# Sliding-window attention with channel mix: the xr mixes of the first batch on GpSimd, re-searched instruction lists, and an earlier bank for the last piece

## The chip, the core and the metric

The kernel runs on one core of a Trainium2 chip. The core has TensorE (PE, whose weight loads appear as PEld), VectorE (DVE), ScalarE (ACT), GpSimd (POOL) and SyncE (SP), which work from their own instruction queues and meet through semaphores. Data goes between HBM and SBUF by DMA; matmul results go to PSUM, which has eight banks here. The metric is the device time in microseconds, as a median of several executions.

## The reference

The inputs q, k and v are [8, 8, 576, 64] (batch, head, position, head dimension). The first stage is causal attention in a window of 128 with ALiBi slopes, the second is an RWKV channel mix with d_model 512 and d_ff 1024.

```python
scores = scale * np.matmul(q, k.transpose(0, 1, 3, 2))
mask = (rel >= 0) & (rel < window)              # rel = query - key, window 128
attn = softmax(np.where(mask, scores + bias, -1e9))   # bias = -slope[head] * |rel|
x = np.matmul(attn, v)                          # -> [8, 576, 512]
x_prev = x shifted down by one position, zeros first
xk = mu_k * x + (1.0 - mu_k) * x_prev
xr = mu_r * x + (1.0 - mu_r) * x_prev
k = np.maximum(xk @ w_k, 0.0)                   # w_k [512, 1024]
v = k * k @ w_v                                 # w_v [1024, 512]
r = 1.0 / (1.0 + np.exp(-(xr @ w_r)))           # w_r [512, 512]
out = r * v
```

(The softmax line is shortened; the reference spells it out.)

## The kernel before

All matmuls are in bf16. A batch has 576 = 4 x 128 + 64 positions; the last 64 are called its tail.

**Attention, batch by batch.** q and k of a batch arrive by GpSimd's DMA queue (tile `cb`, the tails `ts`, the values `vs` and `tv`) and are turned by PE (`qk_quad`, `qk_some`, `tails`, the helper `transpose` at L397), or from batch 4 on by transposing DMAs of SP. ACT or DVE copies the turned blocks from PSUM to `qk`, `tt` or `qx` (`copy_any`, L715). `scores` (L742) multiplies two heads at a time, one in each 64-row half of the array; ACT takes the exponent (L766); the ALiBi factor and the mask are a DVE product with a table (L779), or for the first batch a bias matmul (L748) with the diagonal tiles `sid`. `attend` (matmuls at the helper line L394, `vs` with `at`) also sums the weights through a column of ones; DVE takes the reciprocal (L813) and scales (L819) into `xu`. PE transposes `xu` (L397), and ACT or DVE copies it to `xt` (through `copy_of`).

**`shift`** makes the channel mix's inputs of a head pair g: `dl` = x - x_prev (L906, DVE), then the two mixes `xk` = dl * mu_k + x_prev and `xr` = dl * mu_r + x_prev, each one DVE instruction (scalar_tensor_tensor, L913). Batch 0 is worked in two parts, positions 0 to 256 and 256 to 576, so it has eight xk mixes and eight xr mixes, of 256 and 320 elements a partition. In the first part `dl` of all four head pairs is kept in a spare output buffer (shown as `ot` in the profile), and the xr mixes are made after the last xk mix.

**`channel_mix`** works on two batches (a pair) in slices of columns. For each of eight slices of d_ff, four matmuls with `wk_sb` (a wk group), a relu (L994, ACT or DVE) and a square (L1000 and L1002) give `kk`. For each 128 output rows, four matmuls of 512 columns with `wr_sb` (a wr group) and a tanh on ACT (L1046) give `rs`, then two halves of four matmuls each with `wv_sb` (wv groups, the halves of d_ff) end in one DVE instruction (L1060) that makes `ot`, which SP stores (L1085). The last 128 rows are worked in two pieces of 384 and 128 columns (`FIN`), the second stored by ACT's queue (L1079). Each piece asks for its own PSUM bank when it starts.

**The order of the work.** `Plan` simulates the kernel's nodes (each a few instructions, with a duration, a latency, buffers that it needs and frees). PE, ACT and DVE work through lists written out in `ORDER`; a list's numbers count the nodes of these three engines in the order in which the program creates them, so a node's number in a list also decides which engine makes it where several may. GpSimd and SP take whatever is ready, lowest priority number first; a DMA's priority is its number among all nodes. GpSimd issues the loads (waiting, by the plan, for the eighth load before it to be done). A change between 64-row and 128-row operands on PE has a price of its own in the plan (`SWITCH`). The first loads, after q and k of the first part of batch 0, come in the order of the string below: v is values, K and k the two halves of w_k, a and b q/k of batch 1 and its tail, R w_r, W and w the two halves of w_v, c the values of batch 1; the loads of batch 2 follow.

```python
LOADS = 'v2tKVkabRWwc'
```

`WARM` lists column counts (in units of 128) of PE warm-up matmuls ahead of the first data.

Of the kernel before, what the change touches and what calls it, by code (L numbers as in the profile page):

```python
# [37 lines left out]
""".split()],  # L38
    "ACT": [int(x) for x in """
# [10 lines left out]
""".split()],  # L50
    "DVE": [int(x) for x in """
# [190 lines left out]
def kernel(  # L242
# [35 lines left out]
    WARM = (4, 4, 4, 4, 4, 4, 4, 1, 1)  # L278
# [42 lines left out]
    def XT(b, g):  # L321
        return XT0 if b < 2 else (ACT,)
# [35 lines left out]
    ident = cst.tile([128, 128], BF16, name="ident")  # L358
    mask = cst.tile([128, H, 512], BF16, name="mask")
# [50 lines left out]
    def dve_t(n, fast=1):  # L410
        return (n / fast + 66) / 960.0

    XRL = 4.0

# [370 lines left out]
    def attend(b, g, t0, t1, ha, deps, prio):  # L785
# [43 lines left out]
        r = op(DVE, 0.2, [a], prio + (0,), emit_r, [hx])  # L829
# [5 lines left out]
    def out_t(b, g, t0, t1, hx, deps, prio, hk, ht, late=None):  # L835
# [15 lines left out]
        x = op(XT(b, g), {ACT: act_t(n), DVE: dve_t(n)}, [o, virt_xt[b]], prio + (1,), lambda e: copy_of(  # L851
# [17 lines left out]
    def out_some(b, g, hx, deps, prio, ht):  # L869
# [7 lines left out]
        for r in range(2):  # L877
            nt = NJ - r

            def emit_c(e, r=r, nt=nt):  # L880
                copy_of(hp[r], e, xt_buf[ht.idx][:, g:g + m, X0:X0 + S].rearrange(
                    "p g (t c) -> p g t c", c=64)[:, :, r::2],
                    one(hp[r]).bitcast(BF16)[:, 0:64 * m * NJ].rearrange(
                        "p (g t c) -> p g t c", g=m, c=64)[:, :, 0:nt])
            xs.append(op(XT(b, g), {ACT: act_t(64 * m * nt), DVE: dve_t(64 * m * nt)},
                         [o, virt_xt[b]], prio + (1,), emit_c, (), [hp[r]]))
        return xs

    def shift(b, g, c0, c1, deps, prio, hk, ht, late=None):
# [19 lines left out]
        for i, (buf, mu, nm) in enumerate(((xk_buf, muk_sb, n_muk), (xr_buf, mur_sb, n_mur))):  # L909
            def mix(more=(), i=i, buf=buf, mu=mu, nm=nm):  # L910
                return op(DVE, dve_t(n) + 0.06, [d, nm, virt_x[b // 2]] + list(more),
# [94 lines left out]
    def channel_mix(P, c0, c1, first, xks, xrs, order):  # L1006
# [27 lines left out]
        for i, c in enumerate(range(c0 // 128, c1 // 128)):  # L1034
# [30 lines left out]
            for a, b in ((0, FIN), (FIN, 512)) if final else ((0, 512),):  # L1065
                if a:
                    hv = Hold("p")
# [262 lines left out]
```

## Time and profile before

| | |
|---|---|
| time, median of 3 | 225.93 us (225.9 to 226.34) |
| the profiled execution | 226.01 us, its span 224.0 us |
| granted TensorE clock | 1.00 |
| PE busy | 217.2 us, 97% of the span |
| PEld, DVE, ACT, POOL busy | 126.5, 187.1, 152.3, 92.1 us |
| chain of waits | PE 86%, DMA 8%, POOL 2% |
| DMA | 33.83 MB, 151 GB/s on average |

The span runs from the first to the last instruction that the profiler saw; 2.0 us of the execution lie around it. A line of the profile names the kernel's line, the engine, the operation and the tiles, written one first, and then the count. In the timeline, the first two numbers are the start and the length in us of a run of like instructions; matmuls are pipelined, so the length of a PE run reaches past the start of the next, and PE's prices are best taken from start to start. In the groups, what stands after the bar is the busy time of the group in us, the mean of one instruction in ns, and the idle time of the engine ahead of them with what ended it.

### The profile page before, as it was taken

To read this page: it belongs to the slowest core of one execution; us is meant where nothing else is said; L and a number is where in the kernel's file an instruction comes from. 1 tells how busy PE (TensorE), PEld (TensorE's weight loads), DVE (VectorE), ACT (ScalarE), POOL (GpSimd) and SP (SyncE) were. 2 spreads that over 40 slices of the span, in tenths; PEclk is the share of its full clock that TensorE was granted. 3 is DMA by queue.
4 is the path that set the end of the run, shared out by engine and by line. 5 is a ranking of instruction groups with operands and counts; after the bars stand their busy time and mean duration, and the time that the engine had idled before them with its cause. 6 is when DMAs were issued, how large, how long until landed. Compare 5 with 4: busy or idle time off the path is not lost.

```text
span 224.0 us, 6237 instructions
## 1 busy us (share of the span) xinstructions
PE 217.2 (97%) x2482; PEld 126.5 (56%) x2482; DVE 187.1 (84%) x426; ACT 152.3 (68%) x272; POOL 92.1 (41%) x118
## 2 busy tenths in 40 slices
PE   7899899999999999999999999999999999999994
PEld 2466665755776455557565554457744554574442
DVE  6678899999959999998999896899979999864232
ACT  3679899797989886983889943864448832475111
POOL 8964746589990992475425854300000000000000
PEclk9999999999999999999999999999999999999999
DMA  6999999999999999999999999999982183210243
GB/s 168 176 187 200 197 196 175 227 146 154 199 156 170 111 186 125 180 172 155 167 233 151 155 154 148 156 214 208 133 217 89 41 108 68 82 63 0 94 154 127
DMA packets 132092, 33.83 MB, mean 151 GB/s; under 512 B 119256, under 2 KB 127712, under 8 KB 132064
## 3 DMA queue, kind: packets, MB, share of 16 engines
q0 software_dynamic: 95728, 16.26, 96.0%
q1 hardware_dynamic: 34592, 16.59, 39.8%
q10 hardware_dynamic: 1744, 0.59, 1.1%
q8 instruction: 19, 0.31, 0.6%
q14 instruction: 9, 0.07, 0.1%
HBM read 33.56 MB, written 9.44 MB: 192 GB/s over the span
## 4 chain that ended last, share of the span: by engine, by line
PE 86%; DMA 8%; POOL 2%; ACT 1%; issue 1%; DVE 0%; POOLq 0%; ACTq 0%
PE duo L394 76%; PE duo L742 7%; DMA cb<-in_k_dram 5%; PE duo L397 3%; DMA qx<-in_k_dram 3%; POOL vs L518 1%; ACT qk L715 1%; ACT xt L715 0%; POOL qx L514 0%; POOL cb L514 0%; ACT rs L1046 0%; POOL dist L457 0%; POOL dist L465 0%; POOL dist L468 0%; DVE ot L1060 0%
## 5 line engine op out<-in xcount | busy, mean ns | idle before, releaser
L394 PE MATMUL duo<-xk,wk_sb 128*128 128x256 bf16 (+2 forms) x416 | 69.7, 314 | 0.3 <-DMA wk_sb<-in_moe_w_k_dram 0.3
L394 PE MATMUL duo<-wv_sb,kk 128*128 128x512 bf16 (+2 forms) x296 | 69.9, 374 | 0.1
L766 ACT ACTIVATE at<-duo 128x1024 bf16<-128x1024 f32 (+2 forms) x68 | 64.8, 1008 | 3.3 <-PE duo L742 3.1
L994 ACT ACTIVATE rl<-duo 128x384 bf16<-128x384 f32 (+2 forms) x94 | 42.9, 484 | 28.8 <-PE duo L394 25.1
L394 PEld LDWEIGHTS <-wk_sb 128*128 128x128 bf16 x416 | 38.7, 98 | 21.7 <-issue 0.6
L394 PEld LDWEIGHTS <-kk 128*128 128x128 bf16 x296 | 27.1, 98 | 29.9 <-issue 1.1
L1046 ACT ACTIVATE rs<-duo 128x512 bf16<-128x512 f32 x36 | 21.6, 613 | 27.2 <-PE duo L394 24.2
L779 DVE TENSOR_TENSOR at<-at,mask 128x1024 bf16<-128x1024 bf16 x56 | 37.3, 686 | 0.6 <-ACT at L766 0.6
L518 POOL DMA_DIRECT2D vs<-in_v_dram x32 | 28.4, 904 | 20.2 <-PE duo L394 16.8
L1060 DVE SCALAR_TENSOR_TENSOR ot<-rs,duo 128x512 f32<-128x512 bf16 (+2 forms) x37 | 24.3, 668 | 14.0 <-PE duo L394 8.5
L394 PE MATMUL duo<-wr_sb,xr 128*128 128x512 bf16 x144 | 35.7, 380 | 0.0
L1002 DVE TENSOR_TENSOR kk<-rl 128x256 bf16<-128x256 bf16 (+2 forms) x92 | 29.5, 335 | 6.0 <-ACT rl L994 5.7
L819 DVE TENSOR_TENSOR xu<-duo,rc 128x640 bf16<-128x640 f32 (+2 forms) x36 | 26.5, 743 | 0.3
L913 DVE SCALAR_TENSOR_TENSOR xr<-dl,mu_sb,xt 128x576 bf16<-128x576 bf16 (+1 forms) x32 | 25.0, 781 | 0.0
L913 DVE SCALAR_TENSOR_TENSOR xk<-dl,mu_sb,xt 128x576 bf16<-128x576 bf16 (+1 forms) x32 | 24.4, 780 | 0.1
L394 PEld LDWEIGHTS <-at 128*128 128x128 bf16 x576 | 21.4, 97 | 5.3 <-ACT at L766 0.3
L394 PE MATMUL duo<-vs,at 128*128 128x65 bf16 x512 | 21.8, 193 | 0.1
L394 PEld LDWEIGHTS <-xr 128*128 128x128 bf16 x144 | 13.3, 98 | 13.9
L549 POOL DMA_DIRECT2D cb<-in_q_dram x20 | 17.7, 921 | 4.9 <-DMA cb<-in_k_dram 1.9
L549 POOL DMA_DIRECT2D cb<-in_k_dram x20 | 17.8, 941 | 2.8 <-DMA vs<-in_v_dram 2.8
L906 DVE TENSOR_TENSOR dl<-xt 128x576 bf16<-128x576 bf16 (+1 forms) x32 | 13.6, 438 | 4.7 <-ACT xt L715 2.2
L715 ACT COPY qk<-duo 128x512 bf16<-128x512 bf16 (+1 forms) x32 | 16.0, 580 | 2.0 <-PE duo L397 2.0
(75 smaller groups left out, 177.5 us busy)
## 6 DMA issues: line engine op xcount, KB each, us to landing
out_dram<-ot SPq DMA_DIRECT2D x34, 256.0 KB, 4.8
vs<-in_v_dram POOLq DMA_DIRECT2D x32, 128.0 KB, 9.1
cb<-in_q_dram POOLq DMA_DIRECT2D x20, 128.0 KB, 8.4
cb<-in_k_dram POOLq DMA_DIRECT2D x20, 128.0 KB, 12.8
wk_sb<-in_moe_w_k_dram POOLq DMA_DIRECT2D x2, 512.0 KB, 9.1
cb<-in_q_dram POOLq DMA_DIRECT2D x4, 256.0 KB, 10.0
cb<-in_k_dram POOLq DMA_DIRECT2D x4, 256.0 KB, 10.2
wv_sb<-in_moe_w_v_dram POOLq DMA_DIRECT2D x2, 512.0 KB, 11.6
```

Of the source, the lines that this page charges most:

```text
L394: return use(h, nc.tensor.matmul(*a, **k))
L518: return dma(POOL, 256, issue_t(1024), lambda e: nc.gpsimd.dma_start(out=vs_buf[h.idx][:, j, :, 0:D], in_=v[b, :, 128 * j:128 * j + 128].r ...
L549: return [dma(POOL, 256, issue_t(1024), lambda e, r=r: nc.gpsimd.dma_start(out=cb_buf[h.idx][:, i, r], in_=src[:, :, r]), [g], kind="q") f ...
L715: return (nc.scalar.copy if e == ACT else nc.vector.tensor_copy)(out=out, in_=in_)
L766: lambda e, ah=ah, w=w, hp=hp: nc.scalar.activation(out=ah(), in_=two(hp)[:, :, 0:w], func=AF.Exp, scale=float(scale)), (), [hp])
L779: nc.vector.tensor_tensor(out=a, in0=a, in1=m, op=ALU.mult)
L819: use(hp, nc.vector.tensor_tensor(out=out_, in0=a5()[:, :, :, 0:D], in1=rc[:, :, 0:nt, None].to_broadcast([128, 2, nt, D]), op=ALU.mult), hx)
L913: lambda e: nc.vector.scalar_tensor_tensor(out=buf[hk.idx][:, g, e0 + c0:e0 + c1], in0=dls(), scalar=mu[:, g:g + 1], in1=xc(1), op0=ALU.mu ...
L994: return nc.scalar.activation(out=out, in_=in_, func=AF.Relu, scale=RELU_SCALE)
L1002: nc.vector.tensor_tensor(out=out, in0=in_, in1=in_, op=ALU.mult)
L1046: lambda e, hp=hp, hs=hs: use(hp, nc.scalar.activation(out=rs_buf[hs.idx], in_=one(hp), func=AF.Tanh, scale=0.5), hs), [hs], [hp])
L1060: use(hv, nc.vector.scalar_tensor_tensor(out=ot_buf[ho.idx][:, a:b], in0=rs_buf[hs.idx][:, a:b], scalar=1.0, in1=one(hv)[:, a:b], op0=ALU. ...
```

## The change

1. In `shift`, the eight xr mixes of batch 0 go to GpSimd: a product with mu into a new fp32 buffer `mix32` (128 x 320) and an addition of x_prev. All eight share the one buffer. The plan prices a pair at 0.0033 us an element + 0.4 and gives it the priority 500, that is, behind all DMAs with a lower number and ahead of those above; it isn't tied to the chain of GpSimd's DMAs.
2. All three lists are searched anew. PE's has 378 entries as before; ACT's goes from 277 to 259, DVE's from 426 to 436. Eight numbers fall out (the mixes), so that a new number from 100 on stands for an older one up to eight higher. The lists also move copies to `qk` and `xt`, relus and squares between ACT and DVE.
3. The copies to `xt` may be on either engine in every batch, not in the first two alone.
4. Planner prices: the reciprocal 0.135 us for 0.2, three kinds of copies from PSUM on DVE at the double rate, the cast of the first part on DVE 0.12 us dearer, and between the two halves of a wv product no latency.
5. The last piece's second PSUM bank is taken together with the first one, ahead of the first matmuls (`spare`).
6. The last warm-up entry is 2 for 1.

```diff
 ORDER = {
     "PE": [int(x) for x in """
-39 40 41 42 43 44 45 46 50 52 47 53 64 66 90 88 67 76 91 78 55 79 93 58 37 81 96 161 69 158 107 84 124 104 162
-110 72 111 141 164 113 114 165 127 128 144 145 130 147 148 131 116 167 150 203 197 170 206 133 200 255 119 153
-191 185 136 267 300 194 270 253 188 222 240 273 214 303 258 288 209 228 237 216 261 217 306 291 294 211 225 212
-276 264 219 309 248 297 408 279 231 243 234 411 312 245 394 441 429 246 414 250 396 432 435 251 333 330 324 342
...
+39 40 41 42 43 90 52 50 44 45 46 53 47 64 88 76 66 91 78 79 55 93 154 67 81 58 96 37 69 103 151 84 106 72 155
+100 107 157 109 110 135 119 158 125 141 138 139 112 160 122 142 123 126 195 163 144 189 198 115 128 259 147 131
+247 177 262 292 192 245 280 180 183 186 265 295 206 201 298 250 208 253 220 229 232 283 209 286 211 203 214 256
+268 301 204 400 226 271 235 289 217 421 223 386 403 240 304 406 388 433 237 242 243 424 436 427 238 367 319 325
...
-    WARM = (4, 4, 4, 4, 4, 4, 4, 1, 1)
+    WARM = (4, 4, 4, 4, 4, 4, 4, 1, 2)
...
     def XT(b, g):
-        return XT0 if b < 2 else (ACT,)
+        return XT0
...
+    mix32 = cst.tile([128, 320], FP32, name="mix32")
...
+    XMIX = 500
...
-        r = op(DVE, 0.2, [a], prio + (0,), emit_r, [hx])
+        r = op(DVE, 0.135, [a], prio + (0,), emit_r, [hx])
...
             def mix(more=(), i=i, buf=buf, mu=mu, nm=nm):
+                if b == 0 and i:
+                    def both(e):
+                        nc.gpsimd.tensor_scalar(out=mix32[:, 0:n], in0=dls(), scalar1=mu[:, g:g + 1],
+                                                scalar2=None, op0=ALU.mult)
+                        nc.gpsimd.tensor_tensor(out=buf[hk.idx][:, g, e0 + c0:e0 + c1],
+                                                in0=mix32[:, 0:n], in1=xc(1), op=ALU.add)
+
+                    return plan.add(POOL, n * 0.0033 + 0.4, 0.25, [d, nm, virt_x[0]], (XMIX,), both,
+                                    (), [hd, ht])
...
                 if a:
-                    hv = Hold("p")
+                    hv = spare
+                elif final:
+                    spare = Hold("p")
                 for half in range(2):
                     m = op(PE, NPO * mm(b - a), squares[4 * half:4 * half + 4] +
-                           [n_wv[half], m], place(),
+                           [n_wv[half], (m, 0.0)], place(),
                            lambda e, f=emit2, h=half, a=a, b=b, hv=hv: f(
                                e, 4 * h, 4 * h + 4, a, b, hv),
-                           [hv] if half == 0 else [], [hk])
+                           [hv, spare] if final and not a and half == 0 else
+                           [hv] if not a and half == 0 else [], [hk])
```

More of the change, by code (lines that the diff above doesn't have):

```diff
@@ L850, in out_t @@
         o = op(PE, 0.0565 * (t1 - t0), deps, prio + (1,), emit, [hp], [hx])
-        x = op(XT(b, g), {ACT: act_t(n), DVE: dve_t(n)}, [o, virt_xt[b]], prio + (1,), lambda e: copy_of(
+        x = op(XT(b, g), {ACT: act_t(n), DVE: dve_t(n, 2)}, [o, virt_xt[b]], prio + (1,), lambda e: copy_of(
             hp, e, xt_buf[ht.idx][:, g, X0 + c0:X0 + c1], tp()[:, c0:c1]), (), [hp])
@@ L884, in emit_c @@
                         "p (g t c) -> p g t c", g=m, c=64)[:, :, 0:nt])
-            xs.append(op(XT(b, g), {ACT: act_t(64 * m * nt), DVE: dve_t(64 * m * nt)},
+            xs.append(op(XT(b, g), {ACT: act_t(64 * m * nt), DVE: dve_t(64 * m * nt, 2)},
                          [o, virt_xt[b]], prio + (1,), emit_c, (), [hp[r]]))
@@ L947, in tails_full @@
         g = virtual("tt", [htt])
-        c = [op(DVE, dve_t(512), [t, g], prio + (0,), emit_c, (), [hp])]
+        c = [op(DVE, dve_t(512, 2), [t, g], prio + (0,), emit_c, (), [hp])]
         return htt, c
@@ L1147 @@
                 for i in range(2):
-                    cs.append(op(CAST, {ACT: act_t(256, True), DVE: dve_t(256, 2) + 0.08},
+                    cs.append(op(CAST, {ACT: act_t(256, True), DVE: dve_t(256, 2) + 0.2},
                                  src0[i, g], prio + (0,), lambda e, i=i, g=g: copy_any(
```

71 rows, old and new, of the table ORDER are left out of this document.

## The prediction

> **What bounds the kernel now.** I read the table of windows first, then the waits of TensorE, then its timeline around the places where the two PE lists differ. The windows split the span at 32 and 220 us; the columns are window, length, then busy us (and instructions) of PE, PEld, DVE, ACT and POOL, the granted clock, the DMA share and GB/s.
>
> ```profile
> 0.00:32.00 32.00, 28.32 (x491) 17.62 (x492) 25.00 (x97) 23.98 (x51) 21.45 (x33) 1.00 1.41 188
> 32.00:220.00 188.00, 188.00 (x1984) 108.43 (x1985) 161.27 (x329) 128.03 (x222) 70.68 (x85) 1.00 1.39 145
> 220.00:224.00 4.00, 0.90 (x10) 0.49 (x8) 0.84 (x2) 0.32 (x1) 0.00 (x0) 1.00 0.37 131
> ```
>
> TensorE is busy all 188.00 us from 32 to 220, at clock 1.00. It sat idle for 32.00 - 28.32 = 3.68 us at the start, and the last 4 us are the drain. So the end moves only with the idle time of the start, with waits that appear later, with work that PE gets more of, and with the drain. What DVE, ACT or GpSimd save elsewhere buys nothing by itself. The early waits of PE, largest first (total us, times, longest):
>
> ```profile
> PE duo L394 <- DVE xt L482: 1.0, 1, 1.0
> PE duo L742 <- ACT qk L715: 0.6, 2, 0.3
> PE duo L397 <- DMA cb<-in_k_dram: 0.5, 1, 0.5
> ```
>
> The three give 2.1 us. The attractive reading is: relieve DVE early, and PE gets these back. What a saved microsecond is worth depends on what PE meets next, so here is the stretch of PE's timeline in which batch 0 ends (start, length with the pipeline's end, line, tiles, count).
>
> ```profile
> 32.80 1.04 PE L394 MATMUL duo<-xk,wk_sb 128*128 128x256 bf16 x8
> 33.68 1.03 PE L394 MATMUL duo<-wv_sb,kk 128*128 128x512 bf16 x4
> 34.63 0.34 PE L742 MATMUL duo<-qk 64*128 64x256 bf16 x4
> 34.81 0.19 PE L742 MATMUL duo<-tt,qk 64*128 64x64 bf16 x2
> 34.84 0.19 PE L742 MATMUL duo<-tt 64*128 64x64 bf16 x2
> 34.97 1.04 PE L394 MATMUL duo<-wv_sb,kk 128*128 128x512 bf16 x4
> ...
> 37.65 0.60 PE L394 MATMUL duo<-xk,wk_sb 128*128 128x256 bf16 x4
> 38.09 1.03 PE L394 MATMUL duo<-wv_sb,kk 128*128 128x512 bf16 x4
> ...
> 41.03 1.03 PE L394 MATMUL duo<-wr_sb,xr 128*128 128x512 bf16 x4
> 41.89 0.62 PE L394 MATMUL duo<-vs,at 128*128 128x65 bf16 x15
> ...
> 42.53 0.45 PE L397 MATMUL duo<-ident,cb 64*64 64x64 bf16 x32
> 42.91 0.47 PE L397 MATMUL duo<-ident,xu 64*128 64x64 bf16 x20
> ...
> 45.15 0.39 PE L742 MATMUL duo<-qk 64*128 64x256 bf16 x4
> 45.38 0.46 PE L397 MATMUL duo<-ident,xu 64*128 64x64 bf16 x20
> 45.77 1.04 PE L394 MATMUL duo<-wv_sb,kk 128*128 128x512 bf16 x4
> 46.72 0.39 PE L397 MATMUL duo<-ident,ts 128*128 128x128 bf16 x4
> ```
>
> Prices from these rows, start to start: a 128x256 matmul with wk costs (33.68 - 32.80) / 8 = 0.11 us; four 128x512 ones cost 41.89 - 41.03 = 0.86. A change between 64-row and 128-row operands costs about 0.095: the piece at 34.81 is followed 0.03 later by its like, the one at 34.84 by a 128-row group 0.13 later (0.10 more), and 34.63 - 33.68 - 0.86 = 0.09 the other way.
>
> Three groups in that stretch read data that came by GpSimd's queue. Each pair below is the issue (from the timeline) and the us to landing (from the DMA view of that moment).
>
> ```profile
> 20.98 0.74 POOL L559 DMA_DIRECT2D wv_sb<-in_moe_w_v_dram  x1 [1.34 <-DMA wk_sb<-in_moe_w_k_dram]
> ```
> ```profile
> wv_sb<-in_moe_w_v_dram POOLq DMA_DIRECT2D x1, 512.0 KB, 11.0
> ```
> ```profile
> 32.27 0.78 POOL L514 DMA_DIRECT2D cb<-in_k_dram  x1 [1.78 <-DMA wv_sb<-in_moe_w_v_dram]
> ```
> ```profile
> cb<-in_k_dram POOLq DMA_DIRECT2D x1, 256.0 KB, 9.0
> ```
> ```profile
> 37.62 0.68 POOL L539 DMA_DIRECT2D ts<-in_k_dram  x1
> ```
> ```profile
> ts<-in_k_dram POOLq DMA_DIRECT2D x1, 64.0 KB, 9.0
> ```
>
> The first half of wv lands at 31.98 (used at 33.68), the k quad of batch 2 at 41.27 (used from about 42.72, the second half of the group at 42.53), its tail at 46.62 (used at 46.72, so already tight). The bracketed releasers show that issues wait for earlier landings: loads pace themselves.
>
> **Part one, the PE list.** Both lists hold 378 entries, so PE's work is unchanged but for row changes. Counting them along the lists gives 89 before and 94 after, three of the five before the tail of batch 2: 5 x 0.095 = +0.48 us. Nothing hides that, since PE is saturated.
>
> Gate one, the first wv group. The new list has four wk groups fewer before it (16 x 0.11 = 1.76 us) and one scores piece more (34.63 to about 34.87, 0.24). With the old early waits PE would be there at 33.68 - 1.76 + 0.24 = 32.16, and the weights land at 31.98. So of all the early waits at most about 0.2 us can be gained here; the rest would become a wait for wv. Gate two, the quad of batch 2: fewer before it are the wk group at 37.65 (0.44), the wr group at 41.03 (0.86) and the attend group at 41.89 (about 0.55 before the row change), and there are two row changes more. 42.53 - 0.44 - 0.86 - 0.55 + 0.19 = 40.87, its k half half of 42.91 - 42.53 later, at 41.06, against the landing at 41.27: a wait of 0.21 us. Gains at gate one come back as a longer wait here. Gate three, the tail of batch 2: fewer before it are the wr group, the groups at 45.15 and 45.38 (0.62) and the wv group at 45.77 (0.86); another quad comes ahead of it (0.38). 46.72 - 0.86 - 0.62 - 0.86 + 0.38 + 3 x 0.095 + 0.21 = 45.26, against 46.62: up to 1.36 us of wait, if the tail lands as before.
>
> It should land sooner. The two stores of batch 0's first rows are issued while the tail's transfer is queued:
>
> ```profile
> 36.76 3.49 SPq L1085 DMA_DIRECT2D out_dram<-ot  x2
> ```
>
> In the new lists the second of them comes later, since its wv group is pushed behind the quad. The four loads that end with this tail are 64 KB each, a quarter of a 256 KB store, so a store held back frees about as much as the whole set; I estimate a landing near 45.5, the wait at 0.2 us, and keep 0 and 1.36 as ends.
>
> **Part two, GpSimd.** Eight mixes leave DVE:
>
> ```profile
> L913 DVE SCALAR_TENSOR_TENSOR xr<-dl,mu_sb,xt 128x320 bf16<-128x320 bf16 x4 | 2.2, 546 | 0.0
> ```
> ```profile
> L913 DVE SCALAR_TENSOR_TENSOR xr<-ot,mu_sb,xt 128x256 bf16<-128x256 bf16 x4 | 1.7, 480 | 0.0
> ```
>
> That is 3.9 us off DVE. But the DVE list grows from 426 to 436 entries and ACT's shrinks from 277 to 259, because copies and relus move the other way; in the stretch that matters DVE is left about as full, and ACT, which feeds the second wait above, is eased. PE's own total stays. GpSimd gets 16 instructions instead. Nearest rows:
>
> ```profile
> L457 POOL IOTA dist<- 128x256 bf16 x1 | 0.3, 344 | 0.4 <-POOLq L1314 0.4
> L468 POOL TENSOR_SCALAR_AFFINE_SELECT dist<-dist 128x128 bf16<-128x128 bf16 x1 | 0.3, 339 | 0.0
> ```
>
> They bound one by 0.34 us (256 elements) and 0.34 x 320/128 = 0.85: 5.5 to 13.6 us in all; the code's own price, 0.0033 n + 0.4 for a pair, makes 10.8, which I take. The Trainium skill, "GPSIMD Engine Reference", section on performance versus the Vector engine, gives about 1.03 cycles an element with one input and 2.6 with two, an estimated 7 us for the sixteen; no row here shows the second.
>
> Behind these instructions GpSimd's load issues queue. The priority of a mix is 500, so it goes ahead only of loads numbered above that; a load may be issued up to one pair, 1.5 us, late. Since each lands 9 to 11 us after issue behind others, and the later ones are for work far ahead, I cost that at nothing; with the cover gone, it is 1.5 us at gate two or three. xr is read by the wr group, first due about 32 us, a dozen us after the first part's mixes and late enough for the second's if GpSimd keeps its price.
>
> **Part three, the rest.** WARM adds one warm-up of 256 columns ahead of any data: nothing, as PE waits there anyway. The changed planner prices act only through the lists. The last piece takes its second bank early:
>
> ```profile
> 220.37 0.43 PEld L394 LDWEIGHTS <-kk 128*128 128x128 bf16 x7 [0.31 <-issue]
> ```
> ```profile
> 220.38 0.92 DVE L1060 SCALAR_TENSOR_TENSOR ot<-rs,duo 128x384 f32<-128x384 bf16 x2 [0.88 <-ACT rs L1046]
> ```
>
> The weight loads of that piece stand idle 0.31 us, and most of it would go from PE. But the first of DVE's two last operations waits for the same ACT result and cannot begin sooner than 220.38. The two stretch over 0.92 us; by their 384 and 128 columns I estimate 0.55 and 0.22 us, so at most 0.15 us of idle time lies between them. I take 0.15, ends 0 and 0.31.
>
> Sum: 0.48 + 0.21 + 0.2 - 0.15 = +0.74 us. The profiled execution took 226.01 us, 224.0 of span and 2.0 around it, so it would be 226.75; the median, 225.93, lies 0.08 lower and gives 226.7.
>
> **Rivals.** First, faster: wv, the quad and the tail land earlier than in the old trace, because with the new lists the buffers of the early loads come free and GpSimd issues the next ones sooner. Then the freed waits count in full. From a landing of wv before about 31.4, with the two later gates following, each microsecond counts up to the 2.1 of the three waits; one microsecond turns +0.74 into -0.26 with the gates' 0.41 still there and into about -0.7 without: 225.3. For it: the waits for DVE and ACT are real. Against it: the DMA share is 1.41 of the engines in that window, so the transfers are queued, and nothing puts one earlier in the line. Chance 0.19.
>
> Second, same: gates two and three are loose (each load some tenths sooner), and the row changes less the tail remain, 0.48 - 0.15 = +0.33, 226.3, or less if gate one gives its 0.2: 226.1. Chance 0.23.
>
> Third, much slower: DVE stops while GpSimd reads memory. This trace has one place to look, the small DVE operations beside GpSimd's selects (min/median/max ns):
>
> ```profile
> L686 DVE TENSOR_SCALAR sid<-ident x8: 181/190/242, 1.4 to 6.5; 128x128 bf16<-128x128 bf16 x8
> ```
>
> The slowest took 61 ns over the fastest, too short to tell a lock from a shared port. If DVE lost 0.6 of the 10.8 us, 6.5 us, its saved 3.9 would not cover it, and 2 to 4 us would reach PE as waits for copies and mixes: 229 to 230. The Trainium skill, "SBUF — State Buffer", section "Who interferes with whom", has this rule: the two engines share a port pair under an exclusive lock, and a DVE operation with two inputs from SBUF is blocked for the whole GpSimd instruction. No run here shows it yet. Chance 0.1.
>
> Not a separate case, but in the range: the tail lands as before, and gate three costs its 1.36: 227.9.
>
> **How the numbers follow.** The forecast, with gate three anywhere between its ends, has 0.48: 226.4 to 227.9. The range takes in the same-case and most of the faster one and leaves out the lock: 225.3 to 228.2. About 0.2%, 0.45 us, is what a measurement of this kernel can tell from no change. Faster by more than that: most of the first rival, 0.17. Within: the second and the edges of the first and the forecast, 0.29. Slower: the rest of the forecast and the lock, 0.54.
>
> **What would show it.** Right: in the new profile PE's busy time from 32 to 220 is again near full but for two short waits, on the cb quad of batch 2 and on its ts tail, of some tenths each; xr rows on POOL, 16 of them, 0.35 to 0.9 us each; DVE's xk mixes near 480 and 545 ns still; a gap below 0.1 us ahead of PE's last piece. Wrong: waits for cb, ts and wv all absent and PE's early idle near 2 us (first rival); xk mixes or mask products far over their times where POOL's mixes run (the lock); or PE waiting for xr itself, if a GpSimd instruction takes well over 0.85 us.

## The result, and the profile after

The changed kernel took 233.69 us (median of 4 runs, 232.54 to 234.22) beside 225.98 us for the kernel before: 1.0334 times as long, interval 1.0308 to 1.0359. The forecast was 226.7 and the range ended at 228.2, so the sign was right and the size was not: +7.7 us, not +0.7.

The profiled execution took 232.54 us, its span 230.8 us. First the table of windows (columns as in the prediction):

```profile
0.00:32.00 32.00, 27.69 (x483) 17.17 (x486) 24.60 (x92) 22.77 (x46) 29.42 (x43) 1.00 1.41 188
32.00:60.00 28.00, 23.23 (x381) 13.88 (x387) 25.11 (x48) 19.88 (x34) 27.15 (x31) 0.94 1.76 151
60.00:220.00 160.00, 158.27 (x1551) 91.41 (x1573) 139.42 (x292) 101.70 (x173) 52.10 (x63) 1.00 1.30 139
```

PE was never idle after 32 us before; now it stands idle 28.00 - 23.23 = 4.77 us between 32 and 60, and 4.31 us in place of 3.68 before that. After 60 us it is full again: the 1.73 us that seem to be missing there go with 22 matmuls whose records are missing (1551 against 1573 weight loads). GpSimd is busy 27.15 of 28 us between 32 and 60. What PE waited for after 32 us (us in total, times, longest):

```profile
PE duo L396 <- DVE xk L925: 2.5, 1, 2.5
PE duo L745 <- ACT at L769: 0.9, 1, 0.9
PE duo L396 <- issue: 0.6, 4, 0.2
PE duo L745 <- DVE rl L1007: 0.6, 1, 0.6
```

No DMA stands in it: none of the three gates on which the forecast was built binds. The largest wait is for `xk`, a mix that stayed on DVE. The chain of waits for the stretch from 24 to 40 us says why (start, us, what):

```profile
25.60 1.76 POOL vs L521 x2
27.36 0.02 issue
27.38 1.79 POOL vs L521 x2
29.16 0.69 POOL tv L526
29.85 1.25 POOL mix L916
31.10 0.07 issue
31.18 0.22 POOL xr L918
31.39 0.56 issue
31.95 0.11 POOL cb L517
32.06 0.77 issue
32.83 1.57 POOL mix L916
34.40 0.02 issue
34.42 0.33 DVE dl L909
34.75 1.74 DVE xk L925 x2
```

Read it downwards. GpSimd works in order, so the first mix of the second part starts only at 29.85, behind five load issues. Its two instructions take 2 us and more. There are two `dl` buffers; DVE can't write the fourth `dl` of the part before GpSimd's second product has read the second buffer, which is at 34.40. Then two `xk` mixes follow, 1.74 us for what is 2 x 0.545 otherwise, and PE, which got to that wk group at 34.05, goes on at 36.54.

The loads behind the mixes are late too. The load of batch 2 that GpSimd issued at 34.86 before is now issued at 41.67:

```profile
34.86 0.74 POOL L514 DMA_DIRECT2D cb<-in_q_dram  x1 [1.81 <-DMA wv_sb<-in_moe_w_v_dram]
```
```profile
41.67 0.82 POOL L517 DMA_DIRECT2D cb<-in_q_dram  x1
```

(The first line is of the kernel before, the second of the changed one.)

### The profile page after: what moved, and what is told of

It reads as the page before. It is cut to its first block, busy times and chain, and to the rows that moved or that the text cites. A ratio compares the mean times of both kernels' runs of the same rounds, so it can differ in the third digit from the quotient of the medians.

```text
span 230.8 us, 6233 instructions
## 1 busy us (share of the span) xinstructions
PE 216.7 (94%) x2452; PEld 126.2 (55%) x2482; DVE 192.6 (83%) x436; ACT 146.0 (63%) x254; POOL 108.7 (47%) x134
## 4 chain that ended last, share of the span: by engine, by line
PE 80%; POOL 7%; DVE 5%; issue 3%; DMA 2%; ACT 1%; SPq 1%; DVEq 0%; ACTq 0%; POOLq 0%
PE duo L396 70%; PE duo L745 6%; POOL mix L916 2%; PE duo L399 2%; DMA qx<-in_q_dram 2%; POOL vs L521 2%; DVE xk L925 1%; POOL xr L918 1%; PE duo L751 1%; DVE xr L925 1%; DVE at L782 1%; SPq L571 1%; ACT at L769 1%; DVE ot L1072 1%; DVE dl L909 0%
## 5 line engine op out<-in xcount | busy, mean ns | idle before, releaser
L396 PE MATMUL duo<-wv_sb,kk 128*128 128x512 bf16 (+2 forms) x283 | 67.9, 376 | 0.9 <-issue 0.5
L1006 ACT ACTIVATE rl<-duo 128x384 bf16<-128x384 f32 (+2 forms) x98 | 44.0, 476 | 32.9 <-PE duo L396 25.0
L782 DVE TENSOR_TENSOR at<-at,mask 128x1024 bf16<-128x1024 bf16 x56 | 37.8, 696 | 0.9 <-ACT at L769 0.9
L1014 DVE TENSOR_TENSOR kk<-rl 128x256 bf16<-128x256 bf16 (+2 forms) x98 | 31.1, 333 | 8.2 <-ACT rl L1006 7.9
L1058 ACT ACTIVATE rs<-duo 128x512 bf16<-128x512 f32 x36 | 21.0, 602 | 24.9 <-PE duo L396 23.4
L396 PE MATMUL duo<-wr_sb,xr 128*128 128x512 bf16 x131 | 34.7, 379 | 0.7 <-issue 0.2
L925 DVE SCALAR_TENSOR_TENSOR xk<-dl,mu_sb,xt 128x576 bf16<-128x576 bf16 (+1 forms) x32 | 25.7, 819 | 0.1
L925 DVE SCALAR_TENSOR_TENSOR xr<-dl,mu_sb,xt 128x576 bf16<-128x576 bf16 x28 | 22.6, 806 | 0.0
L745 PE MATMUL duo<-qk 64*128 64x256 bf16 (+1 forms) x136 | 11.8, 261 | 3.4 <-DVE qk L718 1.1
```

Source lines behind the costliest of these rows:

```text
L396: return use(h, nc.tensor.matmul(*a, **k))
L745: nc.tensor.matmul(sa[:, hl, c0:c0 + n], lhsT=kk_, rhs=qq_, start=not bias, stop=True, skip_group_check=True)
L782: nc.vector.tensor_tensor(out=a, in0=a, in1=m, op=ALU.mult)
L925: lambda e: nc.vector.scalar_tensor_tensor(out=buf[hk.idx][:, g, e0 + c0:e0 + c1], in0=dls(), scalar=mu[:, g:g + 1], in1=xc(1), op0=ALU.mu ...
L1006: return nc.scalar.activation(out=out, in_=in_, func=AF.Relu, scale=RELU_SCALE)
L1014: nc.vector.tensor_tensor(out=out, in0=in_, in1=in_, op=ALU.mult)
```

## Experiments

Theory M: the mixes on GpSimd cause the loss. Theory L: the new lists do. In each comparison the kernel before ran beside on the same chip; ratios are to it.

**The mixes back on DVE.** The changed kernel, with the eight mixes inserted into DVE's new list (all numbers in the old counting).

```diff
-                if b == 0 and i:
+                if False:
     "DVE": ... 173 +123 ... 272 +174 ... 308 +157 ... 305 +140 ...   (second part)
```

> The changed kernel with its new lists, but the eight xr mixes of batch 0 back on DVE (inserted in the DVE list in the gaps of the first part and between the mask products of the second). Theory M, that the mixes on GpSimd cause the loss: 226.0 to 227.5 us, no PE wait for xk of 2.5 us, granted clock 1.00. Theory L, that the new lists cause it and the mixes only lie beside: 230 us or more, the wait for xk still over 1.5 us.

Measured: 230.26 us, ratio 1.021 (1.0187 to 1.0234). Neither theory alone: 3.4 us of the loss go, 4.6 stay. PE's wait for xk falls to 1.0 us, and the 0.9 us wait for ACT's exponent stays as it was.

**The old lists with the mixes on GpSimd.**

```diff
+                if b == 0 and i:
+                    def both(e): ...          # as in the change
 ORDER = { the old lists without 100-103, 123, 140, 157, 174 }
```

> The kernel before with its old lists, less the eight xr mixes, which go to GpSimd as in the change (same two instructions, same priority, same price). Theory M: 229 to 234 us, with products of 0.95 us and more, and PE waiting for xk or dl in the second part. Theory L: 225.5 to 226.5 us.

Measured: 236.25 us, ratio 1.0472 (1.0444 to 1.0499): worse than the whole change, and beyond what M expected. DVE's timeline shows the held buffer at its worst:

```profile
25.17 0.28 DVE L1014 TENSOR_TENSOR kk<-rl 128x256 bf16<-128x256 bf16 x1
32.60 0.33 DVE L909 TENSOR_TENSOR dl<-xt 128x320 bf16<-128x320 bf16 x1 [7.16 <-POOL mix L916]
```

DVE stands still for 7.16 us, with all that is queued behind this `dl`. The new lists put other work of DVE there; they were made with GpSimd's mixes in view, though at too low a price for them.

**Only the first part's mixes on GpSimd**, under the new lists, the second part's on DVE.

```diff
-                if b == 0 and i:
+                if b == 0 and i and late is not None:
```

> The changed kernel with only the four xr mixes of the first part (256 elements) on GpSimd, the four of the second part back on DVE. If the second part carries the loss (its mixes hold the two dl buffers and stretch DVE's xk mixes): 226 to 228 us. If the first part's mixes cost as much, by GpSimd's loads being issued late: 229 to 231 us. Theory L: 231 us or more.

Measured: 231.1 us, ratio 1.0249 (1.0194 to 1.0305), against 1.0187 to 1.0234 for the run with all mixes on DVE. The intervals overlap: the medians differ by 0.8 us, but the four executions spread from 230.02 to 233.04, so what the first part's four cost here is not resolved. The second part's carry more: this interval ends just below that of the whole change (1.0308 to 1.0359).

**Four dl buffers**, in the changed kernel.

```diff
-    dl_buf = many(2, [128, S], BF16, "dl")
+    dl_buf = many(4, [128, S], BF16, "dl")
...
-                     xk=2, rl=3, ... xt=2, dl=2, dl0=4,
+                     xk=2, rl=3, ... xt=2, dl=4, dl0=4,
```

> The changed kernel with four dl buffers in place of two, so that DVE's third and fourth dl need not wait for GpSimd's mixes. If the held buffer is the main part: the 1.0 us wait of DVE goes, the PE wait for xk falls from 2.5 to about 1 us or less, and the time to about 230 us. If the shared memory port is the main part: DVE's stretched instructions stay, xk is still 1.5 us late or more, 231.5 to 233 us.

Measured: 233.2 us, ratio 1.0356 (1.0315 to 1.0396), no difference that can be measured, and DVE still waits 1.0 us for a GpSimd mix ahead of a `dl`. The run didn't test what it was made for: the plan hands out the lowest buffer that it believes free, it believes GpSimd's mixes done early, and so the built program has DVE write the first two buffers again. The next run gives each head pair its own.

**Own dl buffers**, in the changed kernel.

```diff
-    dl_buf = many(2, [128, S], BF16, "dl")
+    dl_buf = many(4, [128, S], BF16, "dl")
...
+            if b == 0:
+                return dl_buf[(3, 1, 0, 2)[g]][:, 0:n]
             return dl_buf[hd.idx][:, 0:n]
```

> The changed kernel with a dl buffer of its own for each of the four head pairs of the second part, assigned by hand. (In the run with four dl buffers the plan, which believes GpSimd's mixes done early, handed out the first two again, so nothing was freed.) If the held buffer is a main part under the new lists too: DVE's 1.0 us wait for the GpSimd product goes, PE's wait for xk falls from 2.5 to 1.5 us or less, and the time to 231.5 to 232.7 us. If DVE is late anyway by its stretched instructions: xk still over 2 us late, 233 us or more.

Measured: 232.63 us (median of five, 231.71 to 235.36), ratio 1.0268 (1.0243 to 1.0293): 1.1 us less than the change by the medians, 1.5 by the ratios. DVE's wait for GpSimd is gone, and PE's wait for xk falls from 2.5 to 0.8 us. PE's waits after 32 us:

```profile
PE duo L399 <- DMA cb<-in_q_dram: 1.0, 1, 1.0
PE duo L745 <- ACT at L769: 0.9, 1, 0.9
PE duo L396 <- DVE xk L927: 0.8, 1, 0.8
PE duo L745 <- DVE rl L1009: 0.8, 1, 0.8
PE duo L399 <- DMA cb<-in_k_dram: 0.6, 1, 0.6
```

The held buffer was 1.7 us of the wait for xk. But PE now reaches the cb quad earlier and meets the loads that GpSimd issued late, 1.6 us of waits that the changed kernel did not have: the second loss was hidden behind the first. PE's idle time before 60 us falls only from 9.08 to 3.93 + 4.42 = 8.35 us. How much time own buffers are worth can't be told from what the clock does: this trace is of an execution of 234.4 us at a mean granted clock of 0.991, the three executions at 0.998 and more took 231.71 to 232.63 us, and the one execution at 1.00 of the previous run, with four buffers, took 232.25.

**Everything but lists and mixes**: the old lists, the mixes on DVE, the bank, the warm-up and the prices of the change.

```diff
-                if b == 0 and i:
+                if False:
 ORDER = { the old lists }
```

> Everything of the change except the new lists and GpSimd's mixes: the old lists, the bank of the last piece taken early, the longer warm-up, the other prices. If the new lists carry what remained after the mixes went back to DVE (+4.6 us in the run with the mixes back): 225.3 to 225.8 us here, 0.15 us or so under the kernel before by the earlier bank. If another part of the change carries it: 229 us or more.

Measured: 227.14 us, ratio 1.0064 (1.0043 to 1.0084): 1.4 us slower, which neither case expected. PE's largest waits after 32 us, of which the kernel before had none (the trace is of the longest of six executions, 228.08 us):

```profile
PE duo L746 <- ACT at L770: 0.8, 1, 0.8
PE duo L400 <- DMA cb<-in_k_dram: 0.6, 1, 0.6
```

**The same with one price put back.**

```diff
-        r = op(DVE, 0.135, [a], prio + (0,), emit_r, [hx])
+        r = op(DVE, 0.2, [a], prio + (0,), emit_r, [hx])
```

> The run with the old lists and all the rest of the change but GpSimd's mixes (227.1 us), with one number put back: the plan's price of the reciprocal, 0.2 us for 0.135. If the prices reach the time by dealing the PSUM banks in another way under the same lists, the PE wait of 0.85 us for ACT near 80 us goes, and the time falls by about that, to 225.9 to 226.5 us. If the prices do nothing: 227.1 us again, and the wait stays.

Measured: 225.81 us, ratio 1.0002 (0.9991 to 1.0014), and no PE wait after 32 us at all. So one number of the plan, a price of DVE's reciprocal, is worth 1.3 us with every list fixed. The plan deals buffers at simulated times; with another price the same lists get other banks and buffers, and PE meets ones that aren't free. That the wait for ACT comes from a bank is argued from the plan's code, and the other is a wait for a load; that both go with the price is shown.

**The bank alone**, on the kernel before.

```diff
                 if a:
-                    hv = Hold("p")
+                    hv = spare
+                elif final:
+                    spare = Hold("p")
```

> The kernel before with only the bank of the last piece taken early. The prediction's term: about 0.15 us faster (0 to 0.31), 225.4 to 225.7 us beside 225.7, with PE's gap ahead of the last piece gone. Rival: the earlier hold takes the bank from another piece and the time stays or rises.

Measured: 225.95 us, ratio 1.0009 (0.9993 to 1.0024): no difference that can be measured. The mechanism is there, DVE's two last operations stretch over 0.75 us where they stretched over 0.92, but 0.17 us is less than this measurement resolves:

```profile
220.10 0.75 DVE L1060 SCALAR_TENSOR_TENSOR ot<-rs,duo 128x384 f32<-128x384 bf16 x2 [0.88 <-ACT rs L1046]
```

**Shadow instructions.** The kernel before with its mixes on DVE, and beside them the same sixteen instructions on GpSimd, on constant tiles.

```diff
+                    def both(e):
+                        nc.gpsimd.tensor_scalar(out=mix32[:, 0:n], in0=dist[:, 0:n], scalar1=mu[:, g:g + 1], ...)
+                        nc.gpsimd.tensor_tensor(out=mixb[:, 0:n], in0=mix32[:, 0:n], in1=dist[:, 320:320 + n], op=ALU.add)
+                    plan.add(POOL, n * 0.0033 + 0.4, 0.25, [d, nm, virt_x[0]], (500,), both)
```

> The kernel before, its eight xr mixes still on DVE, and beside them the same sixteen instructions on GpSimd at the same places, but reading constant tiles and writing a scratch tile, so that nobody waits for their results and they hold no buffer. If the data dependence (mixes late, dl buffers held) is what costs: 225.6 to 227 us. If the shared memory or the delay of GpSimd's load issues costs: 228 to 231 us, DVE's two-input instructions stretched by 0.2 to 0.55 us beside the additions.

Measured: 229.75 us, ratio 1.0177 (1.0158 to 1.0196). Nobody reads these results, and still 4 us are lost.

**Writes only**: IOTAs of about the same length together.

```diff
-                        nc.gpsimd.tensor_scalar(...); nc.gpsimd.tensor_tensor(...)
+                        for _ in range(5 if n == 256 else 7):
+                            nc.gpsimd.iota(mixb[:, 0:256], pattern=[[1, 256]], base=0, channel_multiplier=-1, ...)
```

> As the run with the shadow instructions, but GpSimd runs IOTAs of about the same length together, which write SBUF and read nothing. If reading is what stretches DVE, DVE's instructions keep their times (xk 480 and 545 ns) and what is left is the cost of loads issued late: 225.6 to 227 us. If this run loses as much as the shadow run, it is the occupation of GpSimd and its queue, not the memory port.

Measured: 230.74 us, ratio 1.0221 (1.0207 to 1.0236), as much and a little more. PE's largest wait, first with the shadow instructions, then with the writes:

```profile
PE duo L399 <- DMA ts<-in_k_dram: 2.4, 1, 2.4
```
```profile
PE duo L399 <- DMA ts<-in_k_dram: 3.4, 1, 3.4
```

Under the old lists it is GpSimd's queue: while it computes it issues no loads, and PE meets the tail of batch 2 too early. (In both traces the mean granted clock between 32 and 60 us is also down to 0.94.) DVE's times separate the second effect. The mix of 320 elements, in the run with writes, with the shadow instructions, and in the changed kernel:

```profile
L922 DVE SCALAR_TENSOR_TENSOR xk<-dl,mu_sb,xt 128x320 bf16<-128x320 bf16 x4 | 2.1, 545 | 0.0
```
```profile
L923 DVE SCALAR_TENSOR_TENSOR xk<-dl,mu_sb,xt 128x320 bf16<-128x320 bf16 x4 | 2.2, 579 | 0.0
```
```profile
L925 DVE SCALAR_TENSOR_TENSOR xk<-dl,mu_sb,xt 128x320 bf16<-128x320 bf16 x4 | 3.4, 878 | 0.0
```

Writing beside DVE leaves the mix at 545 ns. Reading beside it stretches it, to 878 ns on average in the changed kernel, where both engines do this work at the same time. DVE's whole busy time says the same: 187.1 us in the kernel before, 187.3 with the writes, 189.1 with the shadow instructions. Which instruction is stretched depends on what it lies beside. In the changed kernel the mixes that took twice their time ran beside an addition, GpSimd's instruction with two inputs:

```profile
31.18 0.82 POOL L918 TENSOR_TENSOR xr<-mix,xt 128x320 bf16<-128x320 f32 x1
```
```profile
31.27 1.08 DVE L925 SCALAR_TENSOR_TENSOR xk<-dl,mu_sb,xt 128x320 bf16<-128x320 bf16 x1
```

**Old lists, GpSimd's mixes, four dl buffers.**

```diff
 (the run with the old lists and the mixes on GpSimd)
-    dl_buf = many(2, ...)      dl=2
+    dl_buf = many(4, ...)      dl=4
```

> The old lists with the mixes on GpSimd (236.3 us with two dl buffers, DVE waiting 7.2 us for a GpSimd product before it may write the next dl), now with four dl buffers. If the held buffer is the price under the old lists: the 7.2 us wait goes and the time falls to 227 to 230 us. If the stretched DVE and late loads are the price: 233 us or more.

Measured: 229.1 us, ratio 1.0144 (1.0129 to 1.016): 7.2 us less than with two buffers. Here the held buffer was the price, in part through the clock, which between 32 and 60 us was 0.82 with two buffers and 1.00 with four. What is left is GpSimd's speed and its queue:

```profile
PE duo L396 <- POOL xr L918: 1.9, 1, 1.9
PE duo L399 <- DMA ts<-in_k_dram: 1.1, 1, 1.1
```

**Old lists, only the first part's four mixes on GpSimd.**

```diff
-                if b == 0 and i:
+                if b == 0 and i and late is not None:
 ORDER = { the old lists without 100-103 }
```

> The old lists with only the four xr mixes of the first part on GpSimd (these have four dl buffers of their own, so none is held), the second part's on DVE. If GpSimd's occupation delays the loads in proportion: about 6.5 us of it against 10.6 us of idle time of GpSimd in the first 32 us, so little, 225.6 to 226.8 us. If any mix on GpSimd costs by the stretched DVE instructions: 227.5 us or more.

Measured: 226.74 us, ratio 1.0039 (1.0027 to 1.0052). In the window in which GpSimd has idle time, four mixes cost little, but they do cost: 0.9 us, with an interval clear of no change, and no PE wait after 32 us that shows where.

**One node of PE's list moved**, in the run with the mixes on DVE: the wv group 246 ahead of the scores piece 435.

```diff
-    ... 444 435 246 ...
+    ... 444 246 435 ...
```

> The new lists with the mixes on DVE (230.3 us), with one node of PE's list moved: a wv group of batch 0 stands ahead of the scores piece of batch 2 before which PE waits 0.9 us for ACT's exponent, instead of behind it. If such waits in the new order are what the lists cost: 0.6 to 0.8 us less (0.9 less one pair of row changes), 229.4 to 229.7 us. If PE only meets the same time elsewhere: 230.0 us or more.

Measured: 230.26 us, ratio 1.0198 (1.016 to 1.0237): no gain that can be told. Two executions took 229.4 us, where the first case expected it, and two 231.1 and 231.7, so the run decides nothing. The trace is of the longest, 231.74 us: in it the 0.9 us wait near 55 us is gone, and another, near 48 us, has grown from 0.3 to 1.76 us. PE's row, and DVE's ahead of it:

```profile
48.44 0.39 PE L745 MATMUL duo<-qk 64*128 64x256 bf16 x4 [1.76 <-DVE xu L822]
```
```profile
46.51 0.69 DVE L1072 SCALAR_TENSOR_TENSOR ot<-rs,duo 128x512 f32<-128x512 bf16 x1 [1.76 <-DMA out_dram<-ot]
```

DVE waits for a store to free an output buffer, with PE behind it. Whether the move dealt the buffers anew, or the store took long in this execution alone, isn't shown.

**No mixes at all.** The changed kernel, in which GpSimd only writes zeros to xr of batch 0; the xr of that batch is left out of its output.

```diff
-                        nc.gpsimd.tensor_scalar(out=mix32[:, 0:n], ...)
-                        nc.gpsimd.tensor_tensor(out=buf[hk.idx][:, g, e0 + c0:e0 + c1], ...)
+                        nc.gpsimd.memset(buf[hk.idx][:, g, e0 + c0:e0 + c1], 0.0)
```

> The changed kernel without the xr mixes of batch 0: GpSimd only writes zeros to xr in their place (one MEMSET each), so that neither DVE nor GpSimd has their work; the output of batch 0 is without its xr. What is left is the cost of the lists and the prices alone. If these cost what the run with the mixes on DVE had (230.3 us): 229 to 230.3 us, the waits of 0.5 and 0.9 us near 26 and 55 us still there. If that run was slow only because the eight mixes had to be put into a full DVE list: 226 to 227.5 us.

Measured: 229.38 us, ratio 1.0146 (1.0129 to 1.0163). With nobody doing the mixes' work, the lists and prices alone cost 3.2 us. PE's waits after 32 us, and then the sum row of the windows up to 60 us:

```profile
PE duo L745 <- ACT at L769: 0.9, 1, 0.9
PE duo L745 <- DVE rl L1004: 0.6, 1, 0.6
```
```profile
sum 60.00, PE 54.08 PEld 33.51 DVE 50.20 ACT 44.81 POOL 47.40; mean PE 27.04 PEld 16.76 DVE 25.10 ACT 22.41 POOL 23.70
```

PE is idle 60.00 - 54.08 = 5.92 us without the mixes, 4.31 + 4.77 = 9.08 with them on GpSimd, and 3.68 in the kernel before: 2.2 us for the lists, 3.2 for the mixes. And the same 436 instructions of DVE take 189.4 us here and 192.6 in the changed kernel: GpSimd's mixes stretch DVE's work by 3.2 us in all.

**Forms of GpSimd's instructions**, behind the last load of the kernel before.

```diff
+            nc.gpsimd.tensor_scalar(out=mix32[:, 0:w], in0=dist[:, 0:w], scalar1=muk_sb[:, 0:1], ...)   # and out=mixb
+            nc.gpsimd.tensor_scalar(out=mix32[:, 0:w], in0=dist[:, 0:w], scalar1=0.5, ...)
+            nc.gpsimd.tensor_tensor(out=mixb[:, 0:w], in0=mix32[:, 0:w], in1=dist[:, 0:w], op=ALU.add)  # and in0=dist
```

> The kernel before with fifteen instructions on GpSimd behind its last load, on constant tiles of 128x256: product by a scalar from memory to fp32 and to bf16, product by a constant to fp32, addition of fp32 and bf16, addition of two bf16, three of each. If the product's 0.96 us comes from the fp32 result: the bf16 one is well under it. If from the scalar out of memory: the one by a constant is under it. If neither: all three near 0.96 us, the additions near 0.67 us.

Its one execution took 227.45 us. The timeline has, among the fifteen (the shortest of each kind are taken as the least disturbed by DVE):

```profile
142.62 0.91 POOL L1303 TENSOR_SCALAR mixb<-dist,mu_sb 128x256 bf16<-128x256 bf16 x1
...
153.49 0.92 POOL L1301 TENSOR_SCALAR mix<-dist,mu_sb 128x256 f32<-128x256 bf16 x1
154.39 1.62 POOL L1303 TENSOR_SCALAR mixb<-dist,mu_sb 128x256 bf16<-128x256 bf16 x1
155.98 0.84 POOL L1305 TENSOR_SCALAR mix<-dist 128x256 f32<-128x256 bf16 x1
156.91 0.68 POOL L1307 TENSOR_TENSOR mixb<-mix,dist 128x256 bf16<-128x256 f32 x1
157.66 0.67 POOL L1308 TENSOR_TENSOR mixb<-dist 128x256 bf16<-128x256 bf16 x1
```

Neither the fp32 result (0.92 against 0.91) nor the fp32 source (0.68 against 0.67) matters; a constant saves little (0.84). The product is simply dearer than the addition.

## Why the prediction was wrong

**What held.** The sign, and that the end moves only with what PE loses: most of the loss, 9.08 - 3.68 = 5.4 of 6.8 us of span, is PE idle before 60 us. The tail: DVE's stretch shrank by the 0.17 us that was read out of the old trace as 0.15, too little to measure. The sign was luck in part, since the two gate waits in the sum, 0.21 and 0.2 us, never appeared. And that DVE's saved 3.9 us buy nothing by themselves is not borne out under the new lists: with the mixes on DVE their ratio is 1.021, with nobody making them 1.0146, about 1.4 us.

**The step that failed first** is in the part on GpSimd: "in the stretch that matters DVE is left about as full, and ACT [...] is eased. PE's own total stays." The sum then asked only whether DMAs would be in time, and PE's waits for DVE and ACT in the new order were never looked for. Of those, 0.9 us (for the exponent, at 53.70) and 0.6 us (for a relu, at 36.24) stand in the run without mixes. The lists and prices cost 3.2 us where the sum had 0.48 + 0.21 + 0.2. The waits at the cb quad and the ts tail did not appear, because PE came there late: in the run without mixes at 42.21 and 46.30, where the prediction's walk had 40.87 and 45.26. The 0.48 for row changes was not measured by itself; PE's busy time is 217.2 us before and 217.8 without mixes. **The second step that failed** is larger: the mixes on GpSimd, which the sum cost at nothing, brought the other 4.5 us, by the four ways that follow.

**GpSimd's price** was taken at 10.8 us, with a bound of 13.6. The products took 6.5 + 3.9 = 10.4 us (groups of the changed kernel, busy us and mean ns behind the bar) and the additions 6.0:

```profile
L916 POOL TENSOR_SCALAR mix<-dl,mu_sb 128x320 f32<-128x320 bf16 x4 | 6.5, 1614 | 0.2
...
L916 POOL TENSOR_SCALAR mix<-ot,mu_sb 128x256 f32<-128x256 bf16 x4 | 3.9, 963 | 0.1
```

A product of 256 elements was 0.96 us, above the row-based bound of 0.34 us by a factor of nearly three: IOTA and select were the wrong neighbours. The Trainium skill ("GPSIMD Engine Reference", performance versus the Vector engine) had 1.03 cycles an element for one input and 2.6 for two, an estimated 7 us for the sixteen; the addition's 0.67 us is near its share, an estimated 0.55 us, and the product, which has one input, is over four times its own.

**"A load may be issued up to one pair, 1.5 us, late"** counted one pair. The four pairs of the second part with two loads between them filled GpSimd from 29.85 to 41.67, and the load behind came 6.8 us later than before. In the changed kernel PE had no wait for it, being late itself; with own `dl` buffers it waited 1.6 us for `cb`, and under the old lists 2.4 and 3.4 us for `ts`.

**The rival of the shared memory** had 0.1 and was no tail event. The sign that the prediction named for it came true: DVE's mix rose from 545 to 878 ns, so its xk mixes were late exactly where PE came to need them. The rule of the Trainium skill that was weighed ("SBUF — State Buffer", who interferes with whom) was right on the two-input operations: they are stretched beside GpSimd's reads and, in the run with IOTAs, not beside its writes. That the other engine is blocked for the whole instruction goes further than these runs show: beside GpSimd's products DVE's mask products took from 0.68 us, their usual time, to 0.93. The rival's time, 229 to 230, was short by the lists' share.

**A wait nobody priced** was the held `dl` buffer: 0.98 us of DVE in the changed kernel, where own buffers take 1.7 us off PE's wait for xk and hand most of it on to waits for loads, and 7.16 us under the old lists, where four buffers win 7.2. The prediction listed who waits behind GpSimd's instructions and left out who waits for the buffers that they read.

**"The changed planner prices act only through the lists"** was false: 1.3 us hang on one price with the lists fixed.

**One of the three early waits** that were counted as winnable, the 1.0 us for DVE, lies before the first warm-up matmul in every run. No change to later work could have won it.

How the parts add up is not exact. The run without mixes has 3.2 us; the mixes on GpSimd bring the other 4.5. How these divide among the stretched DVE work, the held buffer and the late loads was not separated further. A part goes with the clock. In the changed kernel's profile the granted clock falls behind the long wait, shown here for 36 to 40 and 40 to 42 us; it is 0.50 in the two us from 39 to 41. The run with four dl buffers dealt by the plan has the same long wait. Its execution at a granted clock of 1.00 took 232.25 us, two at 0.993 took 232.9 and 233.51, one at 0.984 took 234.75; the changed kernel's four lay between 232.54 us at 0.993 and 234.22 at 0.985. From that one execution at 1.00, 6.6 us over its kernel before, I estimate the clock's part of the 7.7 us at about 1. Why the clock falls behind some of these waits and not behind others stays open.

```profile
36.00:40.00 4.00, 2.86 (x18) 1.52 (x18) 3.93 (x7) 1.05 (x2) 3.77 (x4) 0.76 1.37 157
40.00:42.00 2.00, 1.64 (x15) 0.94 (x15) 1.65 (x3) 0.66 (x2) 1.92 (x3) 0.63 0.01 1
```

None of these versions beats the kernel before.

## What to carry to other kernels

An engine that issues the loads is not free because it is idle: work put on it can delay the loads behind it, hold the buffers that it reads, and slow the neighbour that reads memory beside it, so price all three, and price its instructions by a like one, measured. When an order is replaced, walk it with the busy times of every engine that feeds the bound one, not with the transfers alone. And where a plan deals buffers by simulated times, a price is part of the program: change it and the same lists run otherwise.

## What the runs showed of the hardware

A GpSimd product of 128x256 with one tensor input took 0.91 to 0.98 us where it was least disturbed, whatever its result's type (0.84 with a constant for the scalar), and an addition of two tensors 0.67 us, so the operation with fewer inputs is the dearer one. Beside busy DVE work the same product took up to 1.62 us, and a DVE mix of 0.545 us took 1.08 beside a GpSimd addition: both engines pay. IOTAs, which only write, took 356 ns on average and left DVE's mixes at their times.
